# The last expert of a soft-MoE over four TensorE column groups, and its output stored as whole rows

## The chip, the cores and the metric

The kernel runs on one core of one Trainium2 chip. The metric is the device time of one execution in microseconds, as the median of three runs. The profile times below count from the first instruction of the profiled execution.

## What is computed

Chunk-selected causal attention (4 batches, 8 heads, 768 positions, head size 64) feeds a soft mixture of experts. Cut to what matters here, with `x` the attention output as 3072 rows of 512:

```python
logits = x @ phi                         # 3072 x 32: 8 experts, 4 slots each
d = softmax of logits over the rows      # dispatch weights
slot_input = d.T @ x                     # 32 x 512
for e in range(8):
    h = relu(slot_input[e] @ w1[e])      # 4 x 1024
    slot_out[e] = h @ w2[e]              # 4 x 512
c = softmax of logits over the 32 slots  # combine weights
out = c @ slot_out                       # 3072 x 512, float32, 6.29 MB
```

## The kernel before, in words

**Order.** The schedule is written out by hand: each engine runs its instructions in program order, and semaphores link the engines. 16 head pairs go through a software pipeline, one loop turn for each (i = 1 to 15). All loads are issued from POOL's queue, in program order with POOL's own work: keys, queries and values (L145, L150) and sixteen expert matrices `w_sb` of 1 MB each in bf16 (L138), eight of w1 and then eight of w2. The last one is w2 of expert 7; it is issued at the start of turn 15. The stores are issued from SP's queue (L835, L837, L868, L870).

**Combine weights in the loop.** One batch's MoE work is spread over the turns i = 6, 10 and 14, and the last batch is done behind the loop. `moe_comb2` (L460) runs two exponentials on ScalarE (L463) into `c_pad`, 128 rows x 6 tiles x 4 groups of 32 columns: group j holds at columns 0 to 3 the weights of expert j and at columns 4 to 7 those of expert 4 + j; the other 24 columns are zero. L730 does this for the last batch. `moe_ct` transposes `c_pad` into `cT_all` (L488, L496), and `col_sums` multiplies it by a column of ones (L682) for the sum of each row's weights, whose reciprocals (`inv_a`, `inv_b`) scale the output rows.

**Experts.** The slots of expert e sit in a 32-column block of their own (`siT_pad`, `hT_pad`): columns 0 to 3 for experts 0 to 3, 4 to 7 for experts 4 to 7, zero elsewhere. A matmul of 128 x 32 then uses a quarter of TensorE's columns: expert e works in column group j = e % 4 and leaves its result in PSUM rows 32j to 32j + 31. Matmuls of four experts in a row use four groups. `experts_in` (L766) is the first layer, `relu` L773, `hidden_T` L778 and L782, `experts_out` (L800) the second layer into `so_ps[y]`, where y is the half of the 512 output columns (256 each). `zrow` (L750) carries the dispatch sums, and `inv_b[:, :1]` is their reciprocal for each PSUM row.

**The end of the kernel before** (L840 to L870). Expert 7 is alone, so its 16 matmuls all use column group 3:

```python
experts_out([0, 1], [7], [0])             # 8 matmuls: half 0 of expert 7
nc.scalar.activation(so_sb[0], ...)       # L847
experts_out([0], [7], [1])                # 4 matmuls of half 1
half_out(0, 0)                            # two output matmuls, 128 x 256 each (L832)
experts_out([1], [7], [1])                # 4 more of half 1
nc.scalar.activation(so_sb[1], ...)       # L851, on ScalarE too
```

`half_out(m, y)` makes 256 rows by 256 columns: two matmuls with K = 128 against all slots (L832), one scaled on VectorE (x = 0, L823) and one on ScalarE (x = 1, L825), and a store of half rows, that is of runs of 1 KB in DRAM. The order is (0, 0), (1, 0), (0, 1), (1, 1). The first of these goes out as two stores of 128 KB (L835), the others as three of 256 KB (L837). Then m = 2 to 11: two tiles of 128 x 512 (four matmuls, L863), one on each engine, and a 512 KB store of runs of 4 KB (L870); m = 11 goes as two stores of 256 KB (L868). Four half buffers `oh_sb` and five whole ones `o_sb` hold the output until it has landed.

Of the kernel before, what the change touches and what calls it, by code (L numbers as in the profile page):

```python
# [10 lines left out]
F32 = mybir.dt.float32  # L11
BF16 = mybir.dt.bfloat16
ALU = mybir.AluOpType
ACT = mybir.ActivationFunctionType
# [4 lines left out]
CH = 32  # L19
NCHUNK = 24  # L20
NQT = 6
P = 128
# [38 lines left out]
def kernel(  # L61
# [23 lines left out]
    static = ctx.enter_context(tc.tile_pool(name="static", bufs=1))  # L85
# [13 lines left out]
    c_pad = static.tile([P, NQT, 4, CH], BF16, name="c_pad")  # L99
# [3 lines left out]
    w_sb = []  # L103
# [5 lines left out]
    ones_sq = static.tile([P, P], BF16, name="ones_sq")  # L109
# [4 lines left out]
    squad = static.tile([P, 2, 2, NCHUNK], BF16, name="squad")  # L114
    schunk = static.tile([P, 2, NCHUNK, 1], BF16, name="schunk")
    headsel = static.tile([P, 1, 2, 1], BF16, name="headsel")
    ns_t = [static.tile([P, NJ, 2, 2, CH], BF16, name=f"ns_t{i}") for i in range(2)]

    small = ctx.enter_context(tc.tile_pool(name="small", bufs=1))
# [43 lines left out]
        nc.vector.memset(t[:, :, :, D:D + 1], 1.0)  # L163
    for h in range(2):
        nc.vector.memset(headsel[h * 64:(h + 1) * 64, :, h, :], 1.0)

    nc.gpsimd.affine_select(
        out=squad, in_=squad, compare_op=ALU.not_equal, fill=NEG, base=0,
# [3 lines left out]
        out=squad, in_=squad, compare_op=ALU.not_equal, fill=-1.0, base=-NCHUNK,  # L172
# [5 lines left out]
        out=qgrp, in_=qgrp, compare_op=ALU.not_equal, fill=1.0, base=0,  # L178
# [3 lines left out]
        out=caus[:4], in_=caus[:4], compare_op=ALU.is_ge, fill=NEG, base=0,  # L182
# [277 lines left out]
    def moe_comb2(b):  # L460
        lc = st.pop(("lc", b))
        for g in range(2):
            nc.scalar.activation(  # L463
                c_pad[:, :, :, g * SPE:(g + 1) * SPE],
                lc[:, :, g * 16:(g + 1) * 16].rearrange("p t (j s) -> p t j s", j=4), func=ACT.Exp,
            )

    def moe_dispatch(b):
        d_sb = st.pop(("d", b))
# [182 lines left out]
    hT_pad = pads.tile([P, NFG, E, CH], BF16, name="hT_pad")  # L652
# [52 lines left out]
    def cinv(n):  # L705
        return inv_a[:, n:n + 1] if n < BL * NQT else inv_b[:, 1 + n - BL * NQT:2 + n - BL * NQT]
# [4 lines left out]
        lg2, lhsT=mneg.broadcast_to([NS, P]), rhs=rep.broadcast_to([NS, NQT, NS]), start=False, stop=True,  # L711
# [14 lines left out]
    lc = small.tile([P, NQT, NS], F32, name="lc", tag="lc")  # L726
    nc.vector.tensor_tensor(lc, lg1, rm.broadcast_to([P, NQT, NS]), op=ALU.subtract)
    nc.vector.tensor_tensor(si_acc, si_acc, dm.broadcast_to([P, NDG + 1, NS]), op=ALU.mult)
    for g in range(2):
        nc.scalar.activation(  # L730
            c_pad[:, :, :, g * SPE:(g + 1) * SPE],
            lc[:, :, g * 16:(g + 1) * 16].rearrange("p t (j s) -> p t j s", j=4), func=ACT.Exp,
        )
    keep(2)
    moe_dispatch(BL)
    keep(2)
# [58 lines left out]
    def experts_out(fs, es, ys):  # L795
        for y, f in ((y, f) for y in ys for f in fs):
            for fg in range(f * 4, (f + 1) * 4):
                for e in es:
                    g, j = divmod(e, 4)
                    nc.tensor.matmul(  # L800
                        so_ps[y][j * CH:(j + 1) * CH, :], lhsT=hT_pad[:, fg, e, :],
                        rhs=w_sb[E + e][:, fg * Dm + y * HD:fg * Dm + (y + 1) * HD],
                        start=(g == 0 and fg == 0), stop=(g == 1 and fg == NFG - 1),
                    )

    experts_in(0, 0)
    moe_ct(B - 1)
# [3 lines left out]
    hidden_T(0)  # L811
    experts_in(1, 1)
    relu(1)
    NM, NH = B * NQT // 2, 2
    homes = {"sc": p_sc, "tp": p_tp, "at": p_at}
    half_homes = [iter("tp at sc tp".split()), iter("sc tp sc tp".split())]

    def rows(m):
        return out[m * 2 * P:(m + 1) * 2 * P, :].rearrange("(p x) d -> p x d", x=2)

    def scaled(x, o, ps, n):
        if x == 0:
            nc.vector.tensor_scalar_mul(o, ps, cinv(n))  # L823
        else:
            nc.scalar.activation(o, ps, func=ACT.Copy, scale=cinv(n))  # L825

    def half_out(m, y):
        o_sb = op.tile([P, 2, HD], F32, name="oh_sb", tag="oh_sb", bufs=2 * NH)
        for x in range(2):
            tag = next(half_homes[y])  # L830
            o_ps = homes[tag].tile([P, HD], F32, name="oh_ps", tag=tag)
            nc.tensor.matmul(o_ps, lhsT=cT[:, m, x], rhs=so_sb[y], start=True, stop=True)  # L832
            scaled(x, o_sb[:, x, :], o_ps, 2 * m + x)
            if m == y == 0:
                nc.sync.dma_start(out=rows(m)[:, x, :HD], in_=o_sb[:, x, :])  # L835
        if m + y > 0:
            nc.sync.dma_start(out=rows(m)[:, :, y * HD:(y + 1) * HD], in_=o_sb)  # L837

    w_ctx.close()
    op = ctx.enter_context(tc.tile_pool(name="op", bufs=5))  # L840
# [6 lines left out]
    nc.scalar.activation(so_sb[0], so_ps[0], func=ACT.Copy, scale=zinv)  # L847
    experts_out([0], [7], [1])
    half_out(0, 0)
    experts_out([1], [7], [1])  # L850
    nc.scalar.activation(so_sb[1], so_ps[1], func=ACT.Copy, scale=zinv)  # L851
    half_out(1, 0)
    for m in range(NH):
        half_out(m, 1)

    n = 0
    for m in range(NH, NM):
        o_sb = op.tile([P, 2, Dm], F32, name="o_sb", tag="o_sb")
        for x in range(2):
# [5 lines left out]
            scaled(x, o_sb[:, x, :], o_ps, 2 * m + x)  # L865
            n += 1
            if m == NM - 1:
                nc.sync.dma_start(out=rows(m)[:, x], in_=o_sb[:, x, :])  # L868
        if m < NM - 1:
            nc.sync.dma_start(out=rows(m), in_=o_sb)  # L870
# [30 lines left out]
```

## Time and profile before

| | us |
|---|---|
| median of 3 runs | 167.11 (166.45 to 168.35) |
| profiled execution, its own time | 166.89 |
| its span, first to last instruction | 165.2 |
| PE, DVE, ACT, POOL busy | 142.8, 119.9, 122.8, 103.1 |

The page of the profile gives busy times by engine, the span in 40 slices, the DMA queues, the chain of work that ended last (followed back from the last instruction to what released each step), and the costliest groups of instructions. The view of stretches gives, for any stretch, the busy time and the number of instructions of each engine, the granted clock of TensorE, the mean busy share of the 16 DMA engines, and the GB/s that they moved. A group's row reads "engine operation out<-in count: shortest/median/longest ns". Queue q1 carries the stores, q0 the loads, and q8 instructions.

### The profile page before, as it was taken

Reading aid. Unit: us, or ns where it says so; the run is one execution under the profiler, and the core shown is the slowest. Engines: PE = TensorE matmul, PEld = TensorE weight load, DVE = VectorE, ACT = ScalarE, POOL = GpSimd, SP = SyncE. Lnnn points to the kernel's source line nnn. Section 1 sums busy time; section 2 is a strip of 40 time slices with the busy share of each in tenths; the row PEclk is TensorE's granted clock in tenths of the full one; section 3 lists DMA queues with packets and bytes.
Section 4 is the critical chain, followed back from the end, with each engine's and each line's share of the span. In section 5 each row is a group of like instructions: output and inputs, shape, how many; then the busy total and the mean of one; then the engine's idle time right before and its main releaser. Section 6 shows DMA issues by size and latency. Waiting matters only on the chain.

```text
span 165.2 us, 6132 instructions
## 1 busy us (share of the span) xinstructions
PE 142.8 (86%) x2541; PEld 97.6 (59%) x2541; DVE 119.9 (73%) x419; ACT 122.8 (74%) x166; POOL 103.1 (62%) x202
## 2 busy tenths in 40 slices
PE   7986779999999898999999899998989999894500
PEld 2353456766767585677768567675868747552200
DVE  3376988989999979989997999898536521083620
ACT  3668879999999798999989699996886311193510
POOL 6978749979889398878949796768936200000000
PEclk9999999999999999999999999999999999999655
DMA  3999999999999999999999999999999999158995
GB/s 46 148 157 171 207 157 106 171 192 201 203 200 204 201 205 181 211 193 183 209 191 212 193 214 193 208 219 197 203 207 217 211 215 192 28 195 326 408 404 197
DMA packets 41132, 32.94 MB, mean 199 GB/s; under 512 B 26384, under 2 KB 35600, under 8 KB 41104
## 3 DMA queue, kind: packets, MB, share of 16 engines
q0 software_dynamic: 38416, 26.25, 108.0%
q1 hardware_dynamic: 2688, 6.29, 9.9%
q8 instruction: 20, 0.33, 0.7%
q14 instruction: 8, 0.07, 0.1%
HBM read 52.49 MB, written 6.29 MB: 356 GB/s over the span
## 4 chain that ended last, share of the span: by engine, by line
PE 31%; DMA 29%; ACT 18%; DVE 9%; issue 5%; POOL 4%; DVEq 0%; ACTq 0%
DMA w_sb<-in_moe_w_dram 14%; ACT e_sb L321 11%; DMA k_in<-in_k_dram 9%; DMA out_dram<-o_sb 6%; PE sc_ps L297 6%; PE at_ps L349 4%; PE tr_ps L205 4%; PE sc_ps L307 4%; PE warm_ps L197 4%; ACT qT L214 4%; PE xT_ps L371 2%; DVE mx L268 2%; PE ub_ps L256 2%; DVE x_sb L362 1%; POOL e_sb L331 1%
## 5 line engine op out<-in xcount | busy, mean ns | idle before, releaser
L321 ACT ACTIVATE e_sb<-sc_ps 128x1024 bf16<-128x1024 f32 (+1 forms) x96 | 83.1, 917 | 8.1 <-PE sc_ps L307 7.7
L331 POOL TENSOR_SCALAR_AFFINE_SELECT e_sb<-e_sb 128x256 bf16<-128x256 bf16 x96 | 38.4, 419 | 16.2 <-ACT e_sb L321 15.6
L297 PE MATMUL sc_ps<-qT,kT 64*128 64x384 bf16 (+3 forms) x258 | 36.8, 305 | 2.7 <-ACT e_sb L321 1.7
L307 PE MATMUL sc_ps<-nsT,smask 64*128 64x384 bf16 (+2 forms) x294 | 38.1, 284 | 0.1
L349 PE MATMUL at_ps<-v_t,e_sb 128*128 128x65 bf16 x672 | 29.9, 194 | 1.2 <-DVE x_sb L362 1.0
L349 PEld LDWEIGHTS <-e_sb 128*128 128x128 bf16 x672 | 25.4, 98 | 3.6 <-issue 2.1
L268 DVE MAX8 mx<-ub_ps 128x8 f32<-128x8 f32 (+1 forms) x192 | 17.0, 165 | 4.9 <-PE ub_ps L256 4.1
L297 PEld LDWEIGHTS <-kT 64*128 64x128 bf16 x258 | 14.0, 93 | 10.8 <-issue 5.4
L150 POOL DMA_DIRECT2D v_t<-in_v_dram x16 | 16.9, 1053 | 0.7 <-PE ns_ps L279 0.5
L307 PEld LDWEIGHTS <-smask 64*128 64x128 bf16 x294 | 14.9, 94 | 3.8 <-issue 0.6
L223 DVE TENSOR_REDUCE mm<-kT 128x24 bf16<-128x768 bf16 x16 | 15.1, 943 | 2.5 <-ACT kT L214 2.5
L362 DVE TENSOR_TENSOR x_sb<-at_ps,inv 128x768 bf16<-128x768 f32 (+1 forms) x17 | 15.5, 910 | 0.6
L229 DVE TENSOR_REDUCE mm<-kT 128x24 bf16<-128x768 bf16 x16 | 15.1, 943 | 0.0
L214 ACT COPY qT<-tr_ps 128x768 bf16<-128x768 bf16 x16 | 12.8, 800 | 2.5 <-PE tr_ps L205 2.5
L214 ACT COPY kT<-tr_ps 128x768 bf16<-128x768 bf16 x16 | 12.8, 801 | 1.5 <-PE tr_ps L205 1.5
L145 POOL DMA_DIRECT2D k_in<-in_k_dram x16 | 11.7, 734 | 1.1 <-POOLq L885 0.8
L145 POOL DMA_DIRECT2D q_in<-in_q_dram x16 | 11.5, 722 | 0.0
L138 POOL DMA_DIRECT2D w_sb<-in_moe_w_dram x16 | 11.4, 716 | 0.0
L382 DVE COPY xT_sb<-xT_ps 128x768 bf16<-128x768 bf16 (+1 forms) x15 | 8.1, 537 | 3.2 <-PE xT_ps L371 3.2
L863 PE MATMUL o_ps<-so_sb,cT_all 128*128 128x256 bf16 x40 | 6.8, 298 | 3.8 <-DVE o_sb L823 3.5
L205 PE MATMUL tr_ps<-ident,k_in 128*64 128x128 bf16 x192 | 8.7, 229 | 1.1 <-DMA k_in<-in_k_dram 1.1
L256 PE MATMUL ub_ps<-bd,qpn 128*128 128x48 bf16 x192 | 7.8, 183 | 1.3 <-DVE qpn L239 0.9
(125 smaller groups left out, 212.1 us busy)
## 6 DMA issues: line engine op xcount, KB each, us to landing
w_sb<-in_moe_w_dram POOLq DMA_DIRECT2D x16, 1024.0 KB, 14.0
out_dram<-o_sb SPq DMA_DIRECT2D x9, 512.0 KB, 5.3
k_in<-in_k_dram POOLq DMA_DIRECT2D x16, 192.0 KB, 7.0
q_in<-in_q_dram POOLq DMA_DIRECT2D x16, 192.0 KB, 7.3
v_t<-in_v_dram POOLq DMA_DIRECT2D x16, 192.0 KB, 8.5
out_dram<-oh_sb SPq DMA_DIRECT2D x3, 256.0 KB, 4.2
out_dram<-o_sb SPq DMA_DIRECT2D x2, 256.0 KB, 4.8
out_dram<-oh_sb SPq DMA_DIRECT2D x2, 128.0 KB, 1.9
```

The lines of the kernel that those rows point to most:

```text
L145: nc.gpsimd.dma_start(out=t, in_=src.rearrange("h (p g) d -> p h (g d)", p=P))
L150: nc.gpsimd.dma_start(out=v_t[i % NV][:, :, :, :D], in_=v[b, 2 * j:2 * j + 2].rearrange("h (g p) d -> p h g d", p=P),)
L205: nc.tensor.matmul(ps[h * 64:(h + 1) * 64, g, :], lhsT=src[:, h, g * D:(g + 1) * D], rhs=ident, is_transpose=True,)
L214: nc.scalar.copy(t.rearrange("d (p g) -> d p g", g=NQT), st.pop((nm + "ps", i)).rearrange("d g p -> d p g"),)
L223: nc.vector.tensor_reduce(mm[:, 0, 0, :], kT, axis=AX.X, op=ALU.min)
L268: nc.vector.max(mx[:, a, :], ub[:, a, :max(8, 4 * t + 4)])
L297: nc.tensor.matmul(ps[:, h, c:c + w], lhsT=kT[r, kg * P:(kg + 1) * P], rhs=qT[r, qs], start=True, stop=False,)
L307: nc.tensor.matmul(ps[:, h, c + (f - t0) * P:c + (l - t0) * P], lhsT=smask[r, x, kg].rearrange("p a b -> p (a b)"), rhs=nsT[r, (f - x * NJ ...
L321: nc.scalar.activation(e[:, :, :w], st.pop(("scps", i, g))[:, :, :w], func=ACT.Exp, scale=scale)
L331: nc.gpsimd.affine_select(out=e[:, :, c:c + P], in_=e[:, :, c:c + P], compare_op=ALU.is_ge, fill=0.0, base=0, pattern=[[0, 2], [1, P]], ch ...
L349: nc.tensor.matmul(o, lhsT=st["e", i, g][:, h, c:c + P], rhs=v_t[i % NV][:, h, kg, :], start=(kg == 0), stop=(kg == t),)
L362: nc.vector.tensor_tensor(st["x", b][:, t0:t1, 2 * j:2 * j + 2, :].rearrange("p t h d -> p h t d"), at[:, :, :, :D], inv.broadcast_to([P, ...
```

## The change

- Expert 7 leaves `experts_out`. `last_expert_out(y)` runs its eight matmuls of one half in column groups 0 to 3 in turn, by the eight chunks fg of the hidden layer, so that each PSUM row group holds a partial sum. The weights are a 32-column window of `hT_pad` that starts four columns ahead of expert 7's block, so its slots land on rows 8 to 11 of each group.
- The partial sums are added by the output matmul: `spread_c` writes expert 7's combine weights to columns 8 to 11 of all four groups of `c_pad`, with a third exponential on ScalarE after the other two (at the end of `moe_comb2` in turns 6, 10 and 14, and once for the last batch behind L730). `live` is one for rows 0 to 7 of each group and replaces the ones in `col_sums`, so that the copies aren't counted. A copy on POOL repeats expert 7's dispatch sum in `zrow`.
- `so_sb[0]` stays on ScalarE and `so_sb[1]` goes to VectorE; both halves of expert 7 stand ahead of any output matmul.
- The half tiles m = 0 and 1 give way to one whole tile `first` for m = 0, made from four half matmuls; its row 0 goes out as two stores of 128 KB (runs of 1 KB), its row 1 as one of 256 KB (runs of 2 KB). m = 1 to 10 are stores of 512 KB, m = 11 as before. In `first` ScalarE scales half y = 0 and VectorE y = 1; from m = 1 ScalarE takes x = 0 and VectorE x = 1, the reverse of before. `first` and the others share five buffers.

```diff
+    nc.vector.memset(live, 0.0)
+    for j in range(4):
+        nc.vector.memset(live[j * CH:j * CH + 2 * SPE, :], 1.0)
...
+        spread_c(lc)
+
+    def spread_c(lc):
+        lc7 = lc[:, :, NS - SPE:].rearrange("p t (o s) -> p t o s", o=1)
+        nc.scalar.activation(
+            c_pad[:, :, :, 2 * SPE:3 * SPE], lc7.broadcast_to([P, NQT, 4, SPE]), func=ACT.Exp)
...
-                ps[:, n:n + 1], lhsT=c[:, n // 2, n % 2], rhs=ones_sq[:, :1], start=True, stop=True)
+                ps[:, n:n + 1], lhsT=c[:, n // 2, n % 2], rhs=live, start=True, stop=True)
...
+    nc.gpsimd.tensor_copy(
+        zrow[:, :, 2 * SPE:3 * SPE], zrow[:, 3:4, SPE:2 * SPE].broadcast_to([1, 4, SPE]))
...
+    def last_expert_out(y):
+        h = hT_pad.rearrange("p f e c -> p f (e c)")[:, :, (E - 1) * CH - SPE:E * CH - SPE]
+        for fg in range(NFG):
+            j = fg % 4
+            nc.tensor.matmul(
+                so_ps[y][j * CH:(j + 1) * CH, :], lhsT=h[:, fg, :],
+                rhs=w_sb[2 * E - 1][:, fg * Dm + y * HD:fg * Dm + (y + 1) * HD],
+                start=False, stop=(fg >= NFG - 4),
+            )
...
-    experts_out([0, 1], [7], [0])
+    last_expert_out(0)
     nc.scalar.activation(so_sb[0], so_ps[0], func=ACT.Copy, scale=zinv)
-    experts_out([0], [7], [1])
-    half_out(0, 0)
-    experts_out([1], [7], [1])
-    nc.scalar.activation(so_sb[1], so_ps[1], func=ACT.Copy, scale=zinv)
-    half_out(1, 0)
-    for m in range(NH):
-        half_out(m, 1)
+    last_expert_out(1)
+    nc.vector.tensor_scalar_mul(so_sb[1], so_ps[1], zinv)
+
+    first = op.tile([P, 2, Dm], F32, name="first", tag="o_sb")
+    half = {}
+    for y, tags in enumerate((("tp", "tp"), ("sc", "at"))):
+        for x in range(2):
+            half[x, y] = homes[tags[x]].tile([P, HD], F32, name="oh_ps", tag=tags[x])
+            nc.tensor.matmul(half[x, y], lhsT=cT[:, 0, x], rhs=so_sb[y], start=True, stop=True)
+    for x in range(2):
+        for y, scaled in enumerate((scaled_act, scaled_dve)):
+            cols = slice(y * HD, (y + 1) * HD)
+            scaled(first[:, x, cols], half[x, y], x)
+            if x == 0:
+                nc.sync.dma_start(out=rows(0)[:, x, cols], in_=first[:, x, cols])
+    nc.sync.dma_start(out=rows(0)[:, 1], in_=first[:, 1])
...
-    for m in range(NH, NM):
+    for m in range(1, NM):
         o_sb = op.tile([P, 2, Dm], F32, name="o_sb", tag="o_sb")
-        for x in range(2):
-            tag = ("at", "sc", "tp", "sc", "tp")[n % 5]
+        for x, scaled in enumerate((scaled_act, scaled_dve)):
+            tag = ("sc", "tp", "tp", "sc", "at")[n % 5]
```

More of the change, by code (lines that the diff above doesn't have):

```diff
@@ L116 @@
     headsel = static.tile([P, 1, 2, 1], BF16, name="headsel")
+    live = static.tile([P, 1], BF16, name="live")
     ns_t = [static.tile([P, NJ, 2, 2, CH], BF16, name=f"ns_t{i}") for i in range(2)]
@@ L733 @@
         )
+    spread_c(lc)
     keep(2)
@@ L802, in experts_out @@
                         rhs=w_sb[E + e][:, fg * Dm + y * HD:fg * Dm + (y + 1) * HD],
-                        start=(g == 0 and fg == 0), stop=(g == 1 and fg == NFG - 1),
+                        start=(g == 0 and fg == 0), stop=False,
                     )
+    def last_expert_out(y):
[7 more added lines that the diff above has]
+            )
     experts_in(0, 0)
@@ L813, with scaled_act, scaled_dve @@
     relu(1)
-    NM, NH = B * NQT // 2, 2
+    NM = B * NQT // 2
     homes = {"sc": p_sc, "tp": p_tp, "at": p_at}
-    half_homes = [iter("tp at sc tp".split()), iter("sc tp sc tp".split())]
     def rows(m):
         return out[m * 2 * P:(m + 1) * 2 * P, :].rearrange("(p x) d -> p x d", x=2)
[L821 to L828, printed above, removed]
-        for x in range(2):
[L830 to L837, printed above, removed]
+    def scaled_act(o, ps, n):
+        nc.scalar.activation(o, ps, func=ACT.Copy, scale=cinv(n))
+    def scaled_dve(o, ps, n):
+        nc.vector.tensor_scalar_mul(o, ps, cinv(n))
     w_ctx.close()
@@ L845 @@
     experts_out([0, 1], [4, 5, 6], [0, 1])
-    experts_out([0, 1], [7], [0])
+    last_expert_out(0)
     nc.scalar.activation(so_sb[0], so_ps[0], func=ACT.Copy, scale=zinv)
-    experts_out([0], [7], [1])
-    half_out(0, 0)
-    experts_out([1], [7], [1])
-    nc.scalar.activation(so_sb[1], so_ps[1], func=ACT.Copy, scale=zinv)
-    half_out(1, 0)
-    for m in range(NH):
-        half_out(m, 1)
+    last_expert_out(1)
[13 more added lines that the diff above has]
+    nc.sync.dma_start(out=rows(0)[:, 1], in_=first[:, 1])
     n = 0
-    for m in range(NH, NM):
+    for m in range(1, NM):
         o_sb = op.tile([P, 2, Dm], F32, name="o_sb", tag="o_sb")
-        for x in range(2):
-            tag = ("at", "sc", "tp", "sc", "tp")[n % 5]
+        for x, scaled in enumerate((scaled_act, scaled_dve)):
+            tag = ("sc", "tp", "tp", "sc", "at")[n % 5]
             o_ps = homes[tag].tile([P, Dm], F32, name="o_ps", tag=tag)
@@ L864 @@
                     o_ps[:, y * HD:(y + 1) * HD], lhsT=cT[:, m, x], rhs=so_sb[y], start=True, stop=True)
-            scaled(x, o_sb[:, x, :], o_ps, 2 * m + x)
+            scaled(o_sb[:, x, :], o_ps, 2 * m + x)
             n += 1
```

## The prediction

> **What bounds the kernel now.** I read the profile from its end. First the chain of waits of the last 48 us (start, duration, what), with the page's first line.
>
> ```profile
> span 165.2 us, 6132 instructions
> 119.00 23.35 DMA w_sb<-in_moe_w_dram
> 142.40 1.05 PE so_ps L800 x8
> 143.47 0.48 ACT so_sb L847
> 143.99 0.38 PE oh_ps L832 x2
> 147.84 9.64 DMA out_dram<-o_sb x2
> 157.61 0.75 DVE o_sb L823
> ```
>
> Three parts follow each other: the last weights land at 142.36, a short serial chain makes the first output, and stores run to the end. The view of stretches shows what limits the first and the third (columns: stretch, its length, busy us and count for PE, weight loads, DVE, ACT, POOL; clock, DMA share, GB/s).
>
> ```profile
> 60.00:118.00 58.00, 56.02 (x1112) 40.54 (x1109) 52.71 (x190) 53.21 (x73) 47.61 (x94) 1.00 1.37 201
> 119.00:140.00 21.00, 20.05 (x413) 14.22 (x413) 8.81 (x28) 8.89 (x15) 5.98 (x11) 1.00 1.13 210
> 142.00:144.50 2.50, 1.98 (x16) 1.44 (x16) 0.20 (x1) 0.56 (x2) 0.00 (x0) 1.00 0.00 0
> 145.50:146.00 0.50, 0.50 (x5) 0.41 (x5) 0.37 (x2) 0.40 (x2) 0.00 (x0) 1.00 0.47 162
> 146.00:146.50 0.50, 0.50 (x5) 0.31 (x4) 0.50 (x2) 0.50 (x2) 0.00 (x0) 1.00 0.79 270
> 146.50:147.00 0.50, 0.50 (x7) 0.44 (x6) 0.50 (x2) 0.49 (x2) 0.00 (x0) 1.00 0.27 92
> 147.00:147.50 0.50, 0.48 (x6) 0.29 (x4) 0.50 (x2) 0.50 (x2) 0.00 (x0) 1.00 0.83 279
> 148.00:148.50 0.50, 0.47 (x4) 0.39 (x4) 0.50 (x1) 0.50 (x3) 0.00 (x0) 1.00 0.98 332
> 149.50:150.00 0.50, 0.44 (x4) 0.25 (x3) 0.45 (x1) 0.29 (x1) 0.00 (x0) 1.00 0.06 16
> 150.00:163.00 13.00, 3.02 (x14) 1.50 (x13) 3.76 (x5) 3.44 (x5) 0.00 (x0) 0.64 1.01 401
> 163.50:164.00 0.50, 0.00 (x0) 0.00 (x0) 0.00 (x0) 0.00 (x0) 0.00 (x0) 0.50 0.04 16
> ```
>
> The loads keep every DMA engine busy until 140 (a share over 1 means overlapping packets), so the landing at 142.36 is set by bytes, not by when the load was issued. From 150 the stores run at 401 GB/s: bytes again. Between lies the part that can be gained: no transfer at all from 142 to 144.5, and from 145.5 to 150 a rate well below 401.
>
> **The store stage as the last DMA engine sees it.** At 163.5 to 164.0 a share of 0.04 is 0.32 us of a single engine: one engine ends last, at about 163.9, and the others earlier. The queue rows of 147.5 to 149.5 say why.
>
> ```profile
> q1 hardware_dynamic: 650, 0.62, 91.5%
> q8 instruction: 1, 0.02, 3.9%
> 147.84 1.73 SPq L870 DMA_DIRECT2D out_dram<-o_sb x1
> L870 SPq DMA_DIRECT2D out_dram<-o_sb x9: 383/1129/1728, 147.8 to 157.2; - x9
> ```
>
> An instruction fetch of 16 KB took 3.9% of 16 engines for 2 us, that is 1.25 us of one engine. At that moment SP's issue took 1.73 us instead of 0.38, and behind it the other engines ran dry (share 0.06 at 149.5). So I count for the one engine. Its share of 6.29 MB is 393 KB, at 401/1.01/16 = 24.8 GB/s 15.85 us. Runs of 1 KB went at 332/0.98 = 339 GB/s of full share against 397: 1.05 MB of half rows cost 1.05/0.339 - 1.05/0.397 = 0.45 us more. With the fetch, 15.85 + 0.45 + 1.25 = 17.55. First data at 145.75 (0.47 of the slice that ends at 146.0, with some packets overlapping), idle time of 0.10 + 0.37 + 0.08 = 0.55 in the three slices from 146.0 to 147.5: the sum is 163.85, and the row above puts the end at about 163.9. The account closes.
>
> **What the change does, part by part.**
>
> *Expert 7 in four column groups.* The rows of the same matmuls, four groups at a time and alone:
>
> ```profile
> L800 PE MATMUL so_ps<-w_sb,hT_pad x128: 269/273/284, 137.0 to 144.6; 128*32 128x256 bf16 x128
> 137.04 1.05 PE L800 MATMUL so_ps<-w_sb,hT_pad 128*32 128x256 bf16 x32
> 142.40 1.47 PE L800 MATMUL so_ps<-w_sb,hT_pad 128*32 128x256 bf16 x12 [0.69 <-DMA w_sb<-in_moe_w_dram]
> 144.30 0.48 DVE L823 TENSOR_SCALAR oh_sb<-oh_ps,inv_a 128x256 f32<-128x256 f32 x1 [5.08 <-PE oh_ps L832]
> 144.86 0.85 SPq L835 DMA_DIRECT2D out_dram<-oh_sb  x2
> 145.82 1.93 SPq L837 DMA_DIRECT2D out_dram<-oh_sb  x3
> ```
>
> 32 matmuls in four groups took 1.05 us, the time in which 8 ran in one group (the chain's 1.05 x8). So a round of four costs (1.05 - 0.27)/7 = 0.11, with one matmul at 0.27, and eight are 0.11 + 0.27 = 0.38: so_ps[0] is ready 0.67 us sooner, at 142.78. From there the chain is as before: copy 0.48, matmul, scale 0.47 to 0.48, store. The first store is issued at 144.86 - 0.67 = 144.19 and its data starts at 145.75 - 0.67 = 145.08. Gain: 0.67.
>
> *Second half and copies on two engines.* The other eight matmuls follow in rounds 3 and 4 (to 143.0). VectorE's scaling of 128x256 took 0.48, which I take for its copy to bf16, so so_sb[1] is ready at 143.5, beside ScalarE's first scaling. VectorE then finishes its half of row 0 at 144.34; SP is busy until 144.6 with the first store, so nothing waits. This replaces L851, which sat behind expert 7's last matmuls and the first scaling.
>
> *Whole-row stores.* The first two stores took 0.85 us to issue for 256 KB, the next three 1.93 for 768 KB: 308 and 407 GB/s, with the data behind them at 162 to 279. In after, 512 KB are issued by 144.19 + 3 x 0.42 = 145.45, provided that row 1 is scaled (VectorE 144.85, ScalarE 144.6). m = 1 follows at 145.6 after one 0.75 us tile on VectorE, then one store each 0.75 us. These production times are from the rows below.
>
> ```profile
> L823 DVE TENSOR_SCALAR o_sb<-o_ps,inv_a x7: 743/744/751, 146.6 to 153.9; 128x512 f32<-128x512 f32 x7
> L825 ACT ACTIVATE o_sb<-o_ps,inv_a x7: 680/687/697, 146.7 to 153.9; 128x512 f32<-128x512 f32 x7
> ```
>
> A store of 512 KB drains in 1.3 us, so the engines stay ahead from m = 1 on, and the data of the first three stores (0.39, 0.39 and 0.66 us at 128, 128 and 256 KB) covers the issue except for about 0.05 us twice. Idle time falls from 0.55 to 0.10. Only 0.26 MB is left in runs of 1 KB: 0.11 us instead of 0.45. Together a gain of 0.45 + 0.34 = 0.79. The last store and its landing are as before. Five buffers in place of nine make m = 5 wait for `first`, whose stores land long before; five in rotation already fed 401 GB/s.
>
> [...]
>
> *The instruction fetch* stays: both programs have the same number of TensorE instructions, and the boundary falls at the same count, some 26 matmuls ahead of the end, at about 147 in after. Cost unchanged, 1.25 on one engine.
>
> *The third exponentials.* Their rows and the nearest waits:
>
> ```profile
> 49.88 14.25 DMA k_in<-in_k_dram
> L463 ACT ACTIVATE c_pad<-lc x6: 270/282/282, 61.2 to 118.3; 128x96 bf16<-128x96 f32 x6
> 118.45 0.80 ACT L321 ACTIVATE e_sb<-sc_ps 128x768 bf16<-128x768 f32 x1
> 119.79 1.02 ACT L321 ACTIVATE e_sb<-sc_ps 128x1024 bf16<-128x1024 f32 x1 [0.54 <-PE sc_ps L307]
> PE so_ps L800 <- DMA w_sb<-in_moe_w_dram: 0.7, 1, 0.7
> 133.54 0.51 PE L488 MATMUL cT_ps<-ident,c_pad 128*128 128x128 bf16 x6
> 135.14 0.60 ACT L773 ACTIVATE h_sb<-h_ps 128x512 bf16<-128x512 f32 x1 [3.15 <-PE h_ps L766]
> 138.36 0.38 PE L786 MATMUL z_ps<-identf,zrow 1*128 1x1 f32 x2
> DVE schunk L187 <- POOL squad L171: 1.6, 1, 1.6
> ```
>
> Each costs at most 0.28 us of ScalarE. The one of turn 14 delays the e_sb at 118.45, and so that turn's mask on POOL and the last load's issue behind it; the backlog covers that, since the load took 23.35 us from issue to landing. ScalarE had 0.54 us of idle time ahead of its next step. Behind that, TensorE waits 0.69 us for the weights: any delay of turns 10 and 14, at most 2 x 0.28 = 0.56, fits in. If that cover were gone each would cost its 0.28. Turn 6's exponential, at about 61, lies inside the 14.25 us in which the chain waits for keys until 64.1. The last batch's lies in 3.15 us of idle ScalarE, which begins at 135.14 - 3.15 = 131.99; with 0.28 it is written by 132.3, and its reader, the transposes, starts at 133.54. Cost: zero, at most 0.3.
>
> *live and zrow.* Five small memsets at the start, where VectorE waits 1.6 us for POOL; one copy on an idle POOL at 133, read at 138.36. Zero. `col_sums` keeps its form.
>
> **Sum.** 0.67 + 0.79 = 1.46, less zero: the last data at 162.4 and the span at 163.7. The profiled execution took 166.89, so after takes 165.43. That execution is 0.22 under the median of the runs shown (167.11); from the median it would be 165.65. I say 165.4.
>
> **The rivals.**
>
> *The stores pay back the head start.* If the stage is limited by how the engines drain and not by issue (the slow engine still holds SP back, or holes open behind the first three stores), only the 0.67 stays: 166.2. For it speaks that one engine set the end; against it, the holes at 146.5 and 149.5.
>
> *The fetch falls into a harmless place.* If the fetch meets an engine while it waits, or the last weights land without one beside them (TensorE was ready at 141.7, 0.69 us ahead), up to 0.69 or 1.25 more is gained: 164.2 to 164.7. [...] The row with 3.9% and the issue of 1.73 beside it speak against it.
>
> *Slower.* The third exponentials push TensorE past the landing. ScalarE is busy 53.2 of 58 us from 60 to 118, and each added instruction stands between two score exponentials whose buffers TensorE waits for. It decides from 0.69 (cover) + 1.46 (gain) = 2.15 us of delay, four times the 0.56 that the two can cost directly; each would have to cost a missed turn of about 1.4 us. With 1.4 more per turn the time is 166.89 + 2.8 - 0.69 - 1.46 = 167.5.
>
> **Chances.** The forecast has 0.60 (165.0 to 165.8), the harmless fetch 0.18, the stores that pay back 0.16, slower than before 0.06. The range that leaves out 2 in 10 goes from 164.5 to 166.4. The measurement of this kernel can tell about 1% from no change, 1.67 us; faster by over that means below 165.44, just at the forecast. Half of the forecast's 0.60 and the fetch's 0.18, with a little from shorter holes, make 0.51; slower by over 1% would need more than 168.78, a part of the slower case, 0.04; within 1% gets the other 0.45.
>
> **What would show each step right or wrong.** Right: expert 7's first eight matmuls end 0.38 us after their start; the first store is issued 1.8 us after them instead of 2.46; the stretch from the first data has a share near 1 without a hole; the landing of the last weights is at 142.4 and TensorE still waits for it. Wrong: TensorE arrives after the landing (the exponentials), a hole or a long issue on SP within the first 4 us of stores (the drain), or the last data more than 17.3 us behind the first.

## The result, and the profile after

Over 17 runs each, the changed kernel has a median of 166.14 us and the kernel before 167.11. The ratio is 0.9939, with a 95% interval of 0.9915 to 0.9963: a gain of 0.61%, about 1.0 us. That is less than the 1% that the prediction counts as telling, so it falls under "within 1%". The forecast was a gain of 1.46 us (ratio 0.9913), which lies just outside the interval. The profiled execution took 166.11 us. The chain of waits of its last 46 us, with the page's first line:

```profile
span 164.4 us, 6143 instructions
118.10 24.61 DMA w_sb<-in_moe_w_dram
142.75 0.43 PE so_ps L823 x8
143.20 0.48 ACT so_sb L857
143.73 0.98 PE oh_ps L866 x4
146.43 4.66 DMA out_dram<-o_sb
152.04 5.19 DMA out_dram<-o_sb
157.35 0.75 DVE o_sb L847
```

The chain has the same shape as before: last weights, a short serial piece, stores. Expert 7's eight matmuls take 0.43 us here instead of 1.05. The timeline shows the head of the store stage (start, duration, engine, line; in brackets the wait ahead of it).

```profile
142.75 0.62 PE L823 MATMUL so_ps<-w_sb,hT_pad 128*32 128x256 bf16 x16 [1.87 <-DMA w_sb<-in_moe_w_dram]
143.20 0.47 ACT L857 ACTIVATE so_sb<-so_ps,inv_b 128x256 bf16<-128x256 f32 x1 [6.17 <-PE so_ps L823]
143.42 0.48 DVE L859 TENSOR_SCALAR so_sb<-so_ps,inv_b 128x256 bf16<-128x256 f32 x1 [5.03 <-PE so_ps L823]
144.65 0.84 SPq L872 DMA_DIRECT2D out_dram<-first  x2
148.13 1.51 SPq L889 DMA_DIRECT2D out_dram<-o_sb  x1
```

The first store is issued 144.65 - 142.75 = 1.90 us after expert 7's first matmul; before it was 144.86 - 142.40 = 2.46. But one issue still takes 1.51 us, and the stretches and the queues of 147.5 to 149.5 show the same picture as before:

```profile
145.50:146.00 0.50, 0.50 (x5) 0.32 (x4) 0.40 (x1) 0.36 (x1) 0.00 (x0) 0.50 0.78 260
146.00:146.50 0.50, 0.50 (x4) 0.38 (x3) 0.40 (x2) 0.47 (x1) 0.00 (x0) 0.50 0.78 264
146.50:147.00 0.50, 0.50 (x4) 0.38 (x3) 0.50 (x1) 0.33 (x2) 0.00 (x0) 0.50 0.96 369
147.50:149.00 1.50, 1.44 (x14) 1.05 (x12) 1.50 (x3) 1.32 (x3) 0.00 (x0) 1.00 1.03 399
149.50:150.00 0.50, 0.30 (x2) 0.12 (x2) 0.00 (x0) 0.00 (x0) 0.00 (x0) 1.00 0.72 279
162.50:163.00 0.50, 0.00 (x0) 0.00 (x0) 0.00 (x0) 0.00 (x0) 0.00 (x0) 0.50 0.06 25
143.79:147.20 3.41, 3.41 (x17) 2.45 (x17) 2.49 (x5) 2.53 (x5) 0.00 (x0) 0.50 0.43 151
```

The queues:

```profile
q1 hardware_dynamic: 204, 0.77, 96.4%
q8 instruction: 1, 0.02, 4.4%
```

The 16 KB of instructions held one engine for 4.4% of 16 x 2 us, 1.41 us (1.25 before). Behind the long issue the share falls to 0.72, and one engine again ends after the others (0.06 of the last slice). What is better is the start: the three slices from 145.5 have 0.78, 0.78 and 0.96, where before had 0.47, 0.79 and 0.27 (its first data came at 145.74, here at 145.52). The last row is a surprise of its own: TensorE's granted clock is 0.50 for 3.41 us.

The moment at which the last weights land differs between executions (from 140.8 to 144.5 over the profiles of this study, in kernels with the same loads ahead of it; the two with the latest landings, those of rows_only and shift_split, were long executions). So I compare the profiles from expert 7's first matmul on. (This leaves out one thing that the change may touch: by the records of the DMA engines and of the semaphores, the last weights landed 1.02 us behind the last packet of their load in after and in shift_before, and 0.26 to 0.42 behind it in the other ten profiles. It returns below.) The "store stage" below is the time from the first to the last data packet of the stores, and the "tail" the time from expert 7's first matmul to the last packet, both read from the records of the DMA engines.

| kernel | ratio to before [95%] | median us | expert 7 at | first store after | store stage | tail |
|---|---|---|---|---|---|---|
| before | 1 | 167.11 | 142.40 | 2.46 | 18.15 | 21.49 |
| after | 0.9939 [0.9915, 0.9963] | 166.14 | 142.75 | 1.90 | 17.58 | 20.35 |
| split_only | 0.9923 [0.9879, 0.9967] | 166.44 | 140.88 | 1.84 | 17.72 | 20.44 |
| rows_only | 0.9978 [0.9941, 1.0016] | 167.09 | 143.59 | 2.71 | 17.70 | 21.28 |
| shift_before | 0.9999 [0.9967, 1.0032] | 166.89 | 143.23 | 2.46 | 17.46 | 20.79 |
| shift_after | 0.9869 [0.9833, 0.9906] | 165.07 | 143.52 | 1.82 | 16.67 | 19.36 |
| shift_split | 0.9940 [0.9903, 0.9977] | 165.63 | 144.51 | 1.84 | 17.57 | 20.28 |
| shift_half | 0.9956 [0.9914, 0.9998] | 166.43 | 141.83 | 1.83 | 17.41 | 20.10 |
| shift_keep | 0.9924 [0.9882, 0.9965] | 165.74 | 142.50 | 1.84 | 16.57 | 19.28 |
| exp_triple | 0.9953 [0.9911, 0.9995] | 166.14 | 141.69 | 2.01 | 17.32 | 20.20 |
| shift_so1 | 0.9897 [0.9860, 0.9934] | 165.31 | 141.51 | 1.83 | 16.68 | 19.39 |
| late_fill | 0.9913 [0.9885, 0.9940] | 165.34 | 142.52 | 2.39 | 17.38 | 20.63 |

Each ratio is taken against runs of the kernel before on the same chip, so medians of different rows aren't compared with each other.

### The profile page after: what moved, and what is told of

Its sections match the earlier page's. It is cut to its first block, busy times and chain, and to the rows that moved or that the text cites. A ratio compares the mean times of both kernels' runs of the same rounds, so it can differ in the third digit from the quotient of the medians.

```text
span 164.4 us, 6143 instructions
## 1 busy us (share of the span) xinstructions
PE 141.0 (86%) x2541; PEld 97.3 (59%) x2541; DVE 121.8 (74%) x424; ACT 122.9 (75%) x168; POOL 103.0 (63%) x203
## 4 chain that ended last, share of the span: by engine, by line
PE 36%; DMA 24%; ACT 14%; DVE 11%; issue 6%; POOL 4%; DVEq 0%; POOLq 0%; ACTq 0%; SPq 0%
DMA w_sb<-in_moe_w_dram 15%; ACT e_sb L325 10%; PE sc_ps L301 7%; DMA out_dram<-o_sb 6%; PE at_ps L353 6%; PE sc_ps L311 5%; PE tr_ps L209 5%; ACT qT L218 3%; PE xT_ps L375 3%; DMA k_in<-in_k_dram 3%; PE ub_ps L260 2%; DVE x_sb L366 2%; DVE mx L272 2%; DVE qpn L243 1%; PE ub_ps L253 1%
## 5 line engine op out<-in xcount | busy, mean ns | idle before, releaser
L882 PE MATMUL o_ps<-so_sb,cT_all 128*128 128x256 bf16 x44 | 8.0, 332 | 3.7 <-ACT o_sb L844 3.6
L247 DVE TENSOR_SCALAR qpn<-qT 128x768 bf16<-128x768 bf16 x15 | 9.1, 607 | 0.0
```

## The experiments

The theory: the change does what its parts say, and about a third of a microsecond of the gain is lost because the instruction fetch costs more among the whole-row stores than among the half-row stores of before. The rivals: the whole-row stores themselves bring nothing; the half clock holds back the first tiles; the third exponentials or VectorE's copy cost something.

**One part alone.** split_only has expert 7 in four groups, with the exponentials and `live`, but keeps the half-row stores and ScalarE's second copy:

```diff
     last_expert_out(0)
     nc.scalar.activation(so_sb[0], so_ps[0], func=ACT.Copy, scale=zinv)
     last_expert_out(1)
-    nc.vector.tensor_scalar_mul(so_sb[1], so_ps[1], zinv)
...
+    half_out(0, 0)
+    nc.scalar.activation(so_sb[1], so_ps[1], func=ACT.Copy, scale=zinv)
+    half_out(1, 0)
+    for m in range(NH):
+        half_out(m, 1)
```

> Expert 7 in four column groups with the third exponentials, live and zrow; the end stays as before (half tiles, both slot copies on ScalarE). The theory of the prediction, that the two parts add: 0.67 us faster than before, some 0.4%, the first store 1.8 to 1.9 us behind expert 7's first matmul instead of 2.46, and the holes of the half-row stores still there. The rival, that a head start is paid back by the drain of the stores: no faster than before by more than 0.2 us. If the third exponentials cost something it would be less than 0.4 us faster and TensorE would arrive after the last weights.

rows_only is the reverse: expert 7 in one group as before, then the new stores.

```diff
     experts_out([0, 1], [7], [0])
     nc.scalar.activation(so_sb[0], so_ps[0], func=ACT.Copy, scale=zinv)
-    experts_out([0], [7], [1])
-    half_out(0, 0)
-    experts_out([1], [7], [1])
-    nc.scalar.activation(so_sb[1], so_ps[1], func=ACT.Copy, scale=zinv)
-    half_out(1, 0)
-    for m in range(NH):
-        half_out(m, 1)
+    experts_out([0, 1], [7], [1])
+    nc.vector.tensor_scalar_mul(so_sb[1], so_ps[1], zinv)
+    first = op.tile([P, 2, Dm], F32, name="first", tag="o_sb")
...
```

> Whole-row stores and the slot copies on two engines, but expert 7 in one column group as before and no third exponential. If the parts add: about 0.79 us faster than before less what the second half of expert 7 now waits (8 matmuls in one group, 0.9 us, stand ahead of the first output matmul of the second half and beside the first copy), so 0.3 to 0.8 us. The rival, that the row stores bring nothing by themselves because one DMA engine is held by the instruction fetch in any case: within 0.2 us of before.

The timeline of split_only:

```profile
140.88 0.62 PE L823 MATMUL so_ps<-w_sb,hT_pad 128*32 128x256 bf16 x16 [0.31 <-DMA w_sb<-in_moe_w_dram]
142.72 0.85 SPq L858 DMA_DIRECT2D out_dram<-oh_sb  x2
146.36 1.66 SPq L892 DMA_DIRECT2D out_dram<-o_sb  x1
```

The timeline of rows_only:

```profile
143.59 1.91 PE L800 MATMUL so_ps<-w_sb,hT_pad 128*32 128x256 bf16 x16 [1.44 <-DMA w_sb<-in_moe_w_dram]
146.30 0.93 SPq L849 DMA_DIRECT2D out_dram<-first  x2
```

split_only's first store comes 0.62 us sooner than before's, its tail is 1.05 shorter, and the timed gain, 0.77%, is as large as that of the whole change. rows_only gains nothing that can be measured. Its first store is even 0.25 us later (2.71), since all 16 one-group matmuls (1.91 us) now stand ahead of the first output matmul; the stage is 0.45 shorter and that is mostly eaten. With the fetch where it is, then, the split carries the result, and the rows bring nothing that shows: 20.44 to 20.35 in the tail. Of split_only's 1.05 only 0.62 is the shorter chain. The other 0.43 is a shorter store stage with the same stores: the DMA share of the stretch from 1.8 to 5.3 us behind the first data is 1.02 there and 0.83 in before, whose fetch took 1.26 us and split_only's 0.93. Why the one fetch is followed by a hole and the other isn't stays open.

**The fetch, moved.** The prediction puts the fetch at a count of TensorE's instructions. The traces of before and after agree: each has 20 fetches of 16 KB, on average 254 and 252 TensorE instructions apart (single ones 72 to 362), and the last begins when 5031 and 5027 of 5082 have started. Cutting eight of the nine 512-column warm-up matmuls at the start into quarters keeps their work and adds 24 matmuls, each with its weight load: 48 instructions, by which the last fetch should come sooner in the program's course. This was done to before, after and split_only.

```diff
-    warm(9)
+    warm(1)
+    for _ in range(8):
+        for a in range(4):
+            nc.tensor.matmul(warm_ps[:, a, :], lhsT=ones_sq, rhs=ones_sq, start=True, stop=True)
```

> The kernel before, with 8 of the first 9 warming matmuls split in four each at the start (48 more TensorE instructions, the same columns), so that the last two 16 KB instruction fetches of TensorE fall 48 instructions earlier: the last one just behind the wait for the last weights and ahead of the first store, the one before it well ahead of the landing. Theory of the one engine: the store stage loses its 1.25 us, the issue of 1.73 us on SP and the hole behind it go, so 0.7 to 1.3 us faster than before, and up to 0.5 more if the last weights land sooner. Rival, that the fetch merely stands beside a stage limited by all engines: within 0.3 us of before, the long issue still there.

> The changed kernel with the same 48 more TensorE instructions at the start. Theory of the one engine: 1.0 to 1.4 us faster than the changed kernel from the stores, and up to 0.9 more from the landing of the last weights (in the changed kernel's profile their last semaphore came 1.0 us behind its packet, right after a fetch of 0.97 us), so 1.7 to 2.8 us faster than before. Rival: as the changed kernel, 1.0 us faster than before.

> The kernel with the expert split alone, with 48 more TensorE instructions at the start, so that the last instruction fetch falls ahead of the stores. It is to be read against the changed kernel with the same 48 instructions (first data to last data 16.67 us, expert 7 to the last data 19.36). Theory: the whole-row stores are worth 0.6 to 0.8 us once the fetch is out of the way, so here first to last data takes 17.3 to 17.5 us and expert 7 to the last data 20.0 to 20.2. Rival, that whole rows bring nothing and the earlier pair only differed by its fetch: 16.6 to 16.8 and 19.4.

The timeline of shift_after:

```profile
143.52 0.62 PE L829 MATMUL so_ps<-w_sb,hT_pad 128*32 128x256 bf16 x16 [1.63 <-DMA w_sb<-in_moe_w_dram]
145.34 0.88 SPq L878 DMA_DIRECT2D out_dram<-first  x2
```

Its stretches from 147.5 to 151:

```profile
147.50:149.50 2.00, 2.00 (x14) 1.50 (x12) 1.74 (x3) 1.62 (x3) 0.00 (x0) 0.64 1.03 408
149.50:151.00 1.50, 1.34 (x11) 0.91 (x10) 1.18 (x2) 0.80 (x2) 0.00 (x0) 1.00 1.03 407
```

The fetch now starts at 144.50, 0.98 us behind expert 7's first matmul instead of 4.81, and has ended (145.86) ahead of the first data at 146.21. No hole follows, the stretch where after had 0.72 has 1.03, and the stage takes 16.67 us instead of 17.58. The timed ratio, 0.9869 [0.9833, 0.9906], is the best of the study and lies wholly below after's 0.9939 [0.9915, 0.9963]: shift_after beats both kernels. (Two further kernels with the same shift, below, have 0.9924 and 0.9897, and their intervals overlap after's, so 0.9869 may flatter it.) The timeline of shift_before:

```profile
143.23 1.47 PE L806 MATMUL so_ps<-w_sb,hT_pad 128*32 128x256 bf16 x12 [0.58 <-DMA w_sb<-in_moe_w_dram]
145.69 0.84 SPq L841 DMA_DIRECT2D out_dram<-oh_sb  x2
```

And that of shift_split:

```profile
144.51 0.62 PE L829 MATMUL so_ps<-w_sb,hT_pad 128*32 128x256 bf16 x16 [2.15 <-DMA w_sb<-in_moe_w_dram]
146.35 1.02 SPq L864 DMA_DIRECT2D out_dram<-oh_sb  x2
```

The first stores are as late after expert 7's first matmul as in the kernels that they come from (2.46 and 1.84), so within the tail only the store stage can differ. shift_before's tail is 0.70 shorter than before's (20.79 against 21.49), shift_split's only 0.16 shorter than split_only's; neither is faster in the timed runs. Among half-row stores the fetch thus costs 0.16 and 0.70 in the profiles and nothing that the timed runs show; among the whole-row stores of after it costs 0.99.

The stretches show what the 0.70 of before is: 1.8 us from the first data, the 3.5 us behind them, and the end. First before:

```profile
145.74:147.54 1.80, 1.78 (x16) 1.29 (x14) 1.75 (x4) 1.69 (x5) 0.00 (x0) 1.00 0.67 229
147.54:151.04 3.50, 2.82 (x20) 1.78 (x19) 2.41 (x4) 2.25 (x4) 0.00 (x0) 1.00 0.83 294
```

Then shift_before, and its line of stores:

```profile
146.56:148.36 1.80, 1.78 (x16) 1.29 (x14) 1.75 (x4) 1.69 (x5) 0.00 (x0) 1.00 0.67 227
148.36:151.86 3.50, 2.82 (x20) 1.78 (x19) 2.42 (x4) 2.26 (x4) 0.00 (x0) 1.00 1.03 379
163.50:164.00 0.50, 0.00 (x0) 0.00 (x0) 0.00 (x0) 0.00 (x0) 0.00 (x0) 0.50 0.06 25
L876 SPq DMA_DIRECT2D out_dram<-o_sb x9: 398/1142/1172, 148.7 to 157.3; - x9
```

The holes of the half-row stores (0.67) are the same with and without the fetch. The whole difference is the hole behind the fetch: (1.03 - 0.83) x 3.5 = 0.70. The late end of a single engine, which the prediction put down to the fetch, is there without it too: 0.06 of the last slice here, 0.04 in before. And an issue of 1.14 us is usual later on, with the engines full; an issue of that length alone is no loss.

Seen from the stores: with the fetch away, whole rows shorten the tail by 20.28 - 19.36 = 0.92 and the ratio falls from 0.9940 to 0.9869, though the two intervals just touch; with it, by 0.09 and not at all. That the extra warm-up matmuls themselves help is spoken against by shift_before, which has them and gains nothing.

One rival is not shut out. The shift also moves the fetch ahead of the last one. In after and in shift_before that one ended (141.68 and 142.16) as the last packet of the weights went (141.69 and 142.17), and these are the two profiles in which the landing came 1.02 us behind that packet. Counted from this packet to the last data, before has 21.82 us, shift_before 21.86, after 21.41 and shift_after 19.76. So the late landing can have eaten shift_before's 0.70, and a part of shift_after's timed gain over after can come from the landing and not from the stores. With one profile of each this is argued, not shown. The kernels whose weights landed without that delay speak for the stores all the same: among the whole-row kernels, the two with the fetch among the stores (shift_half and exp_triple, below) have tails of 20.10 and 20.20 and ratios of 0.9956 and 0.9953, the three with the fetch ahead of them (shift_after, shift_keep, shift_so1) 19.28 to 19.39 and 0.9869 to 0.9924. (late_fill, whose profile has a stall of its own, is left out here.)

**Half the way.** shift_half adds 24 instructions only.

```diff
-    warm(9)
+    warm(5)
+    for _ in range(4):
+        for a in range(4):
+            nc.tensor.matmul(warm_ps[:, a, :], lhsT=ones_sq, rhs=ones_sq, start=True, stop=True)
```

> The changed kernel with 24 more TensorE instructions at the start in place of 48. The last fetch falls between the two known places (144.5 and 147.6), at about 145.5 to 147, beside the first stores. Theory that the fetch costs what it overlaps: first to last data 17.2 to 17.6 us, as in the changed kernel without the shift (17.58). Rival, that the added warming instructions help by something other than the fetch's place: 16.7, as with 48.

The first two stores in its timeline:

```profile
143.66 1.70 SPq L878 DMA_DIRECT2D out_dram<-first  x2
```

The stretches behind them:

```profile
144.50:145.00 0.50, 0.50 (x5) 0.33 (x4) 0.50 (x2) 0.50 (x2) 0.00 (x0) 1.00 0.73 248
145.00:145.50 0.50, 0.38 (x5) 0.30 (x4) 0.50 (x2) 0.50 (x2) 0.00 (x0) 1.00 0.06 8
```

The fetch (143.9 to 145.0) came sooner than expected and meets the first two stores. Their issue takes 1.70 us instead of 0.84, the other engines run dry at 145, and the tail is 20.10, near after's 20.35 and not shift_after's 19.36. In the timed runs it is at 0.9956, like after. Its interval lies apart from shift_after's: of the three places tried, only the one ahead of the stores helps.

**The half clock.** In after, TensorE waited 1.87 us for the weights and then ran at half clock from 143.79 to 147.20. shift_keep adds six 512-column matmuls into an unused part of PSUM to shift_after, to fill that wait.

```diff
+    for _ in range(6):
+        nc.tensor.matmul(so_t[:, 1, :], lhsT=ident, rhs=w_sb[E][:, :512], start=True, stop=True)
     last_expert_out(0)
```

> The changed kernel with 48 more TensorE instructions at the start and six filling matmuls of 128x512 (1.3 us) between the experts 4 to 6 and expert 7, where TensorE waited 1.6 to 1.9 us for the last weights in the profiles of the changed kernel and then ran at half its clock for 3.4 us. Theory that the wait brings the half clock and that it costs: no stretch of half clock behind expert 7, output matmuls at 0.11 us pitch instead of 0.21, the first store 1.78 us behind expert 7's first matmul, first to last data 16.2 to 16.5 us. Rival, that the half clock is covered by the stores: first to last data 16.6 to 16.7 us. Where the weights land soon after TensorE is ready the filling costs up to 0.6 us.

The six fillers and expert 7 in its timeline:

```profile
141.10 1.47 PE L863 MATMUL so_ps<-w_sb,ident 128*128 128x512 bf16 x6
142.50 0.62 PE L829 MATMUL so_ps<-w_sb,hT_pad 128*32 128x256 bf16 x16
```

The stretch from there on:

```profile
142.50:146.50 4.00, 3.51 (x40) 2.58 (x40) 2.96 (x6) 3.18 (x7) 0.00 (x0) 1.00 0.29 99
```

The clock stayed at 1.00, and the tail fell by 0.08 (19.28 against 19.36); the timed ratio of 0.9924 is no better than shift_after's. Output matmuls were slower at half clock (18 took 3.41 us in shift_after from 145.53, at 0.50, and 2.40 in shift_keep from 146.5, at 1.00), but the stores were the bound by then: going by these two profiles it cost about 0.1 us where the fetch is out of the way. With the fetch among the stores, as in after, it was not tried.

**The third exponentials, three times.** exp_triple runs each of them three times.

```diff
-        nc.scalar.activation(
-            c_pad[:, :, :, 2 * SPE:3 * SPE], lc7.broadcast_to([P, NQT, 4, SPE]), func=ACT.Exp)
+        for _ in range(3):
+            nc.scalar.activation(
+                c_pad[:, :, :, 2 * SPE:3 * SPE], lc7.broadcast_to([P, NQT, 4, SPE]), func=ACT.Exp)
```

> The changed kernel with the third exponential run three times each instead of once, so eight more exponentials of 0.27 us in all, six of them in turns 6, 10 and 14. Theory of the prediction, that each is covered by the wait for loads: within 0.3 us of the changed kernel, that is about 1 us faster than before, and TensorE still waits for the last weights, 0.4 us less than without them for each turn. Rival, that each costs its time: 0.54 us for each of turns 10 and 14, 1.1 us slower than the changed kernel and no faster than before.

Expert 7 in its timeline:

```profile
141.69 0.28 PE L824 MATMUL so_ps<-w_sb,hT_pad 128*32 128x256 bf16 x1
141.81 0.67 PE L824 MATMUL so_ps<-w_sb,hT_pad 128*32 128x256 bf16 x15
```

Its line of stores (shortest, median and longest issue in ns):

```profile
L890 SPq DMA_DIRECT2D out_dram<-o_sb x10: 384/550/1862, 145.1 to 155.7; - x10
```

Eight more exponentials of about 0.27 us (median 0.274 in after) left the ratio at 0.9953, inside after's interval. One point was expected otherwise: TensorE's row has no wait for the last weights any more (they landed at 141.64, while TensorE was still at the experts ahead). That may be the exponentials, but it isn't shown: TensorE was ready for expert 7 at 141.69 here and between 140.53 and 142.36 in the kernels with one exponential in a place. What the run shows is that eight more of them cost nothing that can be measured, and so one in each place costs nothing either. This execution, too, has its fetch among the stores: the longest issue is 1.86 us.

**The second copy on ScalarE.** shift_so1 is shift_after with `so_sb[1]` put back on ScalarE.

```diff
-    nc.vector.tensor_scalar_mul(so_sb[1], so_ps[1], zinv)
+    nc.scalar.activation(so_sb[1], so_ps[1], func=ACT.Copy, scale=zinv)
```

> The changed kernel with 48 more TensorE instructions at the start, and the copy of the second half of the slot output back on ScalarE behind the first. Theory that two engines for the copies matter: ScalarE's first output scaling starts one copy (0.47 us) later, so the first store is issued 2.2 to 2.3 us behind expert 7's first matmul instead of 1.82, and the last data comes 0.3 to 0.5 us later than with the copy on VectorE (19.36), at 19.7 to 19.9. Rival, that the drain of the stores hides it: 19.3 to 19.5.

Its timeline, from the first copy to the first store:

```profile
141.96 0.47 ACT L863 ACTIVATE so_sb<-so_ps,inv_b 128x256 bf16<-128x256 f32 x1 [5.23 <-PE so_ps L829]
142.34 0.47 ACT L865 ACTIVATE so_sb<-so_ps,inv_b 128x256 bf16<-128x256 f32 x1
142.79 0.84 ACT L850 ACTIVATE first<-oh_ps,inv_a 128x256 f32<-128x256 f32 x2
143.34 0.85 SPq L878 DMA_DIRECT2D out_dram<-first  x2
```

The second copy starts 0.38 us behind the first and ends at 142.81, when the first output scaling starts anyway: it fits into the wait for the output matmul. First store 1.83, tail 19.39, ratio 0.9897: nothing changes that can be told. The two engines for the copies are not where the gain is.

**The fetch moved from the other end.** late_fill puts 24 matmuls of one column into the wait for the last weights instead of into the warm-up.

```diff
+    for _ in range(24):
+        nc.tensor.matmul(so_t[:, 1, :1], lhsT=ident, rhs=w_sb[E][:, :1], start=True, stop=True)
     last_expert_out(0)
```

> The changed kernel with 48 more TensorE instructions in another place: 24 filling matmuls of one column between experts 4 to 6 and expert 7, where TensorE waits for the last weights. They move the last instruction fetch as the 48 at the start did and leave everything ahead of them alone. Theory that the gain came from the place of the last fetch: no issue over 1.2 us among the first stores, expert 7 to the last data 19.3 to 19.6 us, and 1.5 to 2.2 us faster than before. Rival, that the finer warming at the start did it: 20.3 us and as the changed kernel, 1.0 us faster than before.

Its timeline, from expert 7 to the first stores:

```profile
142.52 0.62 PE L823 MATMUL so_ps<-w_sb,hT_pad 128*32 128x256 bf16 x15
143.84 0.27 PE L823 MATMUL so_ps<-w_sb,hT_pad 128*32 128x256 bf16 x1 [0.70 <-issue]
144.91 1.66 SPq L874 DMA_DIRECT2D out_dram<-first  x2
```

This one is inconclusive. The timed ratio, 0.9913 [0.9885, 0.9940], points the way of the theory. But in its profiled execution TensorE stood still for 0.70 us before expert 7's last matmul, waiting for nothing that the profile shows, the fetch fell at 144.88 beside the first stores (two issues in 1.66), and the tail was 20.63. That execution took 166.15 us against the median of 165.34, so the profile does not show what the timed runs do.

## Why the prediction was right and where it was wrong

The median of 166.14 lies inside the range of 164.5 to 166.4 but above the forecast's own 165.0 to 165.8. That the total came this near is partly luck, as its parts did not come as forecast: in the timed runs the split alone gave 0.77%, about 1.3 us where 0.67 was forecast, and the rows added nothing to it where 0.79 was.

*What bounds the kernel, and the chain to the first store: right.* Expert 7's first eight matmuls took 0.43 us (0.38 forecast), and the first store followed 1.90 us after their start, where 1.8 was the sign and 2.46 the value before. The term of 0.67 came out at 0.56 in after and 0.62 to 0.64 in six others with the split.

*The zero terms: right as far as tried.* Three times as many exponentials cost nothing that can be measured, and the copy on VectorE changed nothing in shift_after. `live` and the copy into `zrow` were not taken out alone.

*Whole-row stores: right in size, but only without the fetch.* With the fetch ahead of the stores the stage shortens from 17.46 (shift_before) to 16.67 (shift_after), 0.79 us, which is the term of the forecast; that it is so to the hundredth is luck, as shift_split's 17.57 would make it 0.90. The whole tail then shortens by 20.79 - 19.36 = 1.43 against the forecast's 1.46. In the kernels as they are, the stage goes from 18.15 to 17.58, by 0.57, and is longer than the 17.3 that the forecast set as its sign of being wrong.

*The step that failed: "Cost unchanged, 1.25 on one engine", and with it the 0.79 of the rows in the kernels as they are.* The fetch came where it was forecast (147.56, forecast about 147). Its cost was neither 1.25 nor the same on both sides: against the same kernel with the fetch moved, it was 21.49 - 20.79 = 0.70 us in before and 20.35 - 19.36 = 0.99 in after. Nor was it one engine's in before: the 0.70 is the hole of all engines behind the fetch (share 0.83 instead of 1.03 over 3.5 us), and the late single engine is there without the fetch as well. So the account that closed at 163.85 against 163.9 closed by luck; it charged the fetch with an end that the stores have anyway. In after the same stretch lost less, from 147.32 to 150.82 with a share of 0.93 against 1.02 in shift_after, or 0.32 us; most of the rest of the 0.91 by which its stage is longer came at the end, where its engines finish further apart: over the last 2.31 us the share is 0.51 in after and 0.72 in shift_after, about 0.5 us.

Of the forecast's 1.46 the tail shows 1.14: 0.11 is missing in the chain (0.56 for 0.67) and 0.22 in the stage (0.57 for 0.79). The difference of 0.29 between the two costs of the fetch is the same lack seen from the other side, not a second proof of it, and the profiles with the fetch among whole-row stores differ by nearly as much (tails of 20.10 to 20.35). That a fetch costs more among whole-row stores than among half-row ones is supported by the timed runs (0.9939 to 0.9869 when it moves, against 1 to 0.9999 and 0.9923 to 0.9940), with the landing as a rival, and its cause stays open. A fetch ahead of the data, as the one at 144.50 in shift_after, left no hole behind it (share 1.03), and split_only's cost 0.16; among the stores of before and after it cost 0.70 and 0.99.

*The rivals.* "The stores pay back the head start" (166.2) gave the time nearest to the profiled 166.11, and of its reasons the hole behind the first three stores is the one found, behind the fetch; it was only partly so, as 0.57 of 0.79 remained of the stage. The harmless fetch did not happen in after, but shift_after comes near its price: 1.25 was the most that it gave, and shift_after is 0.99 shorter than after in the tail and 0.0070 lower in the ratio, about 1.2 us. The slower case did not show.

*What stays open.* In the timed runs the fetch seems to cost before nothing (0.9999, where 0.70 us less would be 0.9958, outside the interval of shift_before). The late landing of shift_before's weights would account for it, but one profile of each kernel does not tell how often a run has the fetches, or the landing, in the place that its profile shows. The prediction's reading that bytes alone set the landing holds up to the last packet; what the landing then waited for in after and shift_before is not settled.

## What to carry to other kernels

When several gains are added up, look at what each meets on its way: here the whole-row stores showed their 0.79 us only with an instruction fetch out of their way. A kernel that ends in stores should be read for instruction fetches among them, and instructions added far ahead can move such a fetch: 24 more at the start brought after's from 4.81 us behind expert 7's first matmul to about 2, and 48 to 0.98. The 48 took after from 0.9939 to 0.9869, and did nothing for before. An account that closes isn't thereby right: take the event away, as shift_before does, and see whether the end that it was charged with goes too. Undo each part alone before a gain is put down to all of them: here the split of the last expert alone gave the whole timed gain.

## What the runs showed of the hardware

- One fetch of 16 KB held its DMA engine for 0.88 to 1.26 us in before and 0.89 to 1.40 in after (20 fetches each). When it met stores, a store's issue on SP took 1.28 us in shift_half, 1.51 in after, 1.66 in split_only, 1.73 in before and 1.86 in exp_triple (0.86 in rows_only), where the first two took 0.38 and 0.42 in before. Later issues of 512 KB took up to 1.17 us without a fetch, with the engines full (median 1.14 in shift_before).
- Packets of 1 KB took 47.8 ns and packets of 4 KB 164.0 in before: 343 against 400 GB/s over 16 engines.
- TensorE's granted clock was 0.50 for 3.41 us from 143.79 in after, 1.04 us behind the end of a wait of 1.87, and from 145.53 in shift_after, 2.01 behind one of 1.63. Twelve output matmuls took 2.77 us in after from 144.50; behind a wait of 2.15 in shift_split, twelve took 2.75. Behind the waits of 0.31 to 1.44 us of before, split_only, rows_only, shift_before, shift_half and shift_so1, and in shift_keep, whose wait was filled with matmuls, the first 9 to 30 at the same place took 0.14 to 0.16 us each.
- Two copies of 128x256 on ScalarE, 0.47 us each, started 0.38 us apart (141.96 and 142.34): they overlap.
